# Local attention and two feed-forward networks on one core: the copies of the values all on GpSimd, other transfer costs in the plan, stores held behind attention's loads, and VectorE allowed to take differences

## The chip, the cores and the metric

One core of one Trainium2 chip runs the kernel. The metric is the device time of one execution in microseconds (us); lower is better. Times of one kernel are given as the median of several runs, and one further execution is recorded by the profiler.

## The reference, cut to what is computed

```python
# attention: batch 4, heads 8, 512 local and 32 global tokens, head_dim 64, window 32
s_g = scale * q_g @ k_all.T          # global queries see every key
out_g = softmax(s_g) @ v_all
s_ll = where(|i - j| <= 32, scale * q_l @ k_l.T, -1e9)
a_l = softmax(concat(scale * q_l @ k_g.T, s_ll))
out_l = a_l @ concat(v_g, v_l)
x = concat(out_g, out_l) as 2176 rows (tokens) of 512 (heads x head_dim)
# two networks, d_model 512, d_ff 2048
h = x @ w_in;  x = (h * cos(h)) @ w_out
h = max(x @ w2_in, 0);  out = (h * h) @ w2_out
```

The weights come as eight-byte floats (the kernel reads each as two 32-bit words), all else as four-byte floats.

## The kernel before, in words

**Attention.** Sixteen pairs of heads (pair p belongs to group p // 2, that is four heads of one batch). For each pair TensorE transposes keys and queries (tiles `tk`, `tq`), multiplies scores (`s`), transposes the probabilities (`tw`, and `tg` for the part of the global keys) and multiplies them with the values: first `o<-vgz` (global values), then `o<-va` and `o<-vb` in turn, line 459. The queries of 64 rows see a window of 128 keys, so half of the windows start in the middle of a 128-row block. `va` holds a group's values as loaded; `vb` holds the same values shifted by 64 rows, so that those windows lie at partition 0. `copy_v` makes `vb` from `va`: two copies of 64 x 1024 elements. For groups below `GVB` GpSimd makes them (line 288, rows `vb<-va`), for the others two transfers in the SyncE queue (line 252). `va` and `vb` have two buffers each, so group g waits until group g-2 is done. The gathers `pg<-pt` (line 412) also run on GpSimd; `tg` waits for them.

**Networks.** Each product is done with two-part numbers: a rounded high part (`ACTIVATE`, ScalarE) and the low part, the difference of value and high part (`split`, line 147, a `TENSOR_TENSOR` with both inputs in SBUF). Such differences are made of x (`xs`), of the weights (`wi`, `wo`) and of the middle values (`g`). There are 48 steps, each of 256 of d_ff and a block of 640 or 768 tokens: seven products `ha`, `hb`, `he` (line 820, a Strassen scheme), four middle values named a, d, e, b, then the jobs `y` (line 912), which need the high and low parts of g; the first jobs of a step need d and e. 24 steps belong to each network. At the start of each network the seven operands of each block of tokens are made (sums `xr`, line 683, and their parts `xs`) and stored to DRAM (line 706), from where later steps load them (line 711). The weights of a block come as `raw`, are converted (lines 115 to 138, on GpSimd, ScalarE and VectorE) and split.

**Who decides the order.** The order of attention on TensorE is a table written by hand. Everything else is placed by a planner inside the kernel: every operation is an `Op` with the engines that may do it and a duration on each, and a loop takes, engine by engine, the one that can start and has the earliest due time `latest` ("Q" is the queue of transfers, SyncE). The engines then run their instructions in the order thus written; an instruction that waits holds back all behind it on its engine or queue. `opG` makes an operation of GpSimd alone, `opVG` one for GpSimd or VectorE, whichever the planner finds earlier:

```python
    def opVG(n, fn, *needs):
        if beside[0]:
            return Op({"G": 0.1 + n * 0.0026, "V": 0.2 + n * 0.002}, ...)
```

`made_early` are the networks' operations that the planner may place within attention.

Of the kernel before, what the change touches and what calls it, by code (L numbers as in the profile page):

```python
# [20 lines left out]
P = 128  # L21
# [6 lines left out]
def kernel(  # L28
# [45 lines left out]
    V, A, G = nc.vector, nc.scalar, nc.gpsimd  # L74
# [173 lines left out]
    def copy_v(gi, eng="Q"):  # L248
        va, vb = VA[gi % 2], VB[gi % 2]
        for dst, src in ((vb[0:64], va[64:128, 0:4]), (vb[64:128], va[0:64, 1:5])):  # L250
            if eng == "Q":
                nc.sync.dma_start(dst, src)
            else:
                copy(eng, dst, src)
# [467 lines left out]
    d_g2 = lambda n: 0.1 + n * 0.00235  # L722
# [33 lines left out]
    def opG(d, fn, *needs):  # L756
        return Op({"G": d}, lambda e: fn(), *needs)

    def opVG(n, fn, *needs):
        if beside[0]:  # L760
            return Op({"G": 0.1 + n * 0.0026, "V": 0.2 + n * 0.002}, lambda e: fn(V if e == "V" else G), *needs)
        o = Op({"G": d_g2(n), "V": d_v2(n)}, lambda e: fn(V if e == "V" else G), *needs)
        o.port = "GV"
        return o
# [28 lines left out]
    class Step:  # L793
# [42 lines left out]
        def unit(self, ready, key, f, th):  # L836

            n, s = self.n, self.s
            h = lambda: self.hold(key)
            j, free = cr_ring.next()  # L840

            def new_r():
                self.r[key] = pools["s"].tile([P, 384], F32, tag=f"cr{j}", name="cr")[:, 0:n]
                return self.r[key]

            def ck():
                t = pools["s"].tile([P, 384], I32, tag=f"ck{i}", name="ck")
                self.r["k" + key] = t[:, 0:n]
                A.activation(self.r["k" + key], h(), AF.Copy, bias=0.25, scale=INV2PI)

            def cr():
                V.scalar_tensor_tensor(  # L852
                    new_r(), h(), INV2PI, self.r["k" + key], op0=ALU.mult, op1=ALU.subtract
                )

            def sin():
                A.activation(self.r[key], self.r[key], AF.Sin, bias=halfpi, scale=TWOPI)  # L857

            def relu():
                A.activation(new_r(), h(), AF.Relu)  # L860

            def gg():
                V.tensor_tensor(self.r[key], h(), self.r[key], op=ALU.mult)  # L863

            def ghi():
                if (s, f) not in GT:
                    GT[s, f] = [
                        pools["g"].tile([P, 768], F32R, tag=f"g{f}{i}{s % 2}", name=f"g{i}")
                        for i in range(2)
                    ]  # L870
                A.activation(GT[s, f][0][:, th * n : th * n + n], self.r[key], AF.Copy)  # L871

            def glo(eng):
                hi, lo = GT[s, f]
                c = slice(th * n, th * n + n)
                split(eng, lo[:, c], self.r[key], hi[:, c])

            if self.net == 0:
                i, kfree = ck_ring.next()
                o = opA(d_act(n), ck, ready, *kfree)  # L880
                o = opV(d_ps(n), cr, o, *free)
                ck_ring.free[i] = [o]
                o = opA(d_act(n) + 0.12, sin, o)
            else:
                o = opA(d_act(n), relu, ready, *free)
            o = opV(d_ps(n), gg, o)
            bank_free[self.bank[key]] = o
            o = opA(d_act(n), ghi, o, close_l, *g_free.get(s - 2, []))
            o = opG(d_g2(n), lambda: glo(G), o)
            cr_ring.free[j] = [o]  # L890
            self.half[key] = o

# [243 lines left out]
    q_in, q_at = {}, {}  # L1136
# [11 lines left out]
    def dma(fn, n, kb, *needs):  # L1148

        o = Op({"Q": 0.53 * n}, fn, *needs)  # L1150
        o.dmas = [kb / 205.0] * n
        return o

    def soft(fn, *needs):
# [5 lines left out]
    def opE(on, fn, *needs):  # L1160
        return Op(on, fn, *needs)
# [34 lines left out]
    def copy_vals(gi):  # L1196
        o, free = q_in["v", gi], vb_free.get(gi - 2, [])
        if gi < GVB:
            q_in["vb", gi] = Op({"G": 2.6}, lambda e: copy_v(gi, e), o, *free)
        else:  # L1200
            q_in["vb", gi] = dma(lambda e: copy_v(gi), 2, 256, o, *free)

# [94 lines left out]
    def scores(p):  # L1297
        x, r = pairs[p], p % 3
        main, wins, glob, fst, *qe = X[p]
        kt_free[r] = []  # L1300
        s = opP("S", 1.07, x.s_mm, main, wins, glob, *qe, *(o for k in s_bank.values() for o in k))
        qt_free[r] = [s]
        ep_ops.append(s)
        kt_free[r] = [s, fst]
        x.pg_op = {}
        slots = {}
        for hb in range(2):
            slots[hb] = tw_pt.next()
        for k in s_bank.values():
            k.clear()  # L1310
        kpg, fpg = pg_ring.next()
        x.pt_slot, x.pg_slot, x.pgs = {hb: slots[hb][0] for hb in range(2)}, kpg, PG[kpg]
        for hb in range(2):
            x.pt[hb] = PT[slots[hb][0]]
        x.st_slot, st_free = st_ring.next()
        x.st = ST[x.st_slot]
        todo = [(hb, i, h) for hb, i in ROUNDS for h in range(2)]
        exps = {0: [], 1: []}
        for hb, i, h in todo:
            done = soft(lambda: None, s)  # L1320
            done.lag = 0.27 * (ROUNDS.index((hb, i)) + 1)
            o = opE({"V": 0.245}, lambda e, a=(hb, i, h): x.top(*a), done, *slots[hb][1], *st_free)
            s_bank[UNIT[hb, i, h][0]].append(o)
            ep_ops.append(o)
            exps[hb].append(opE({"A": 0.411}, lambda e, a=(hb, i, h): x.exp(*a), o))
        x.rc = opE({"V": 0.42}, lambda e: x.recip(), *exps[0], *exps[1])
        x.exps = exps
        for hb in range(2):
            x.pg_op[hb] = opE({"G": 0.38}, lambda e, hb=hb: x.gather(hb), *exps[hb], *fpg)

    def p_tr(p, hb):

# [98 lines left out]
    def join(*ops):  # L1431
        return Op({"N": 0.0}, lambda e: None, *ops)

    GVB = 4

    ORDER = (
# [116 lines left out]
    for o in made_early:  # L1553
        o.latest -= 40
        if "Q" in o.on and hasattr(o, "raw"):
            o.latest -= 30

    missing = {o.key: len(o.needs) for o in allops}
    ready = {e: [] for e in "PVAGQN"}
# [19 lines left out]
    def best(e):  # L1579
# [20 lines left out]
                return (tw, w) if tw <= tp + 0.1 else (tp, p)  # L1600
            return (tp, p) if tp <= tw + 0.3 else (tw, w)
        f = free_at[e]
        if not ready[e]:
            return None
        t = max(f, min(o.at for o in ready[e]))
        can = [o for o in ready[e] if o.at <= t]
        o = min(can, key=lambda o: (o.latest, o.key))
        if e in "VAG":
            if not o.att:
# [31 lines left out]
        return t, o  # L1641

    port, lanes, way = [0.0], [0.0] * 8, [17.0]
    SLACK = 1.0
    BIAS, EARLY, LOOK, drift = 6.0, -100, 1, [0.0]
    count = len(allops)
    while count:
        picks = [(b[0], e, b[1]) for e in ready for b in [best(e)] if b]
# [8 lines left out]
        if e == "Q":  # L1657


            f = t  # L1660
            for d in o.dmas:
                f = max(f, lanes.pop(0)) + 0.53
                way[0] = max(way[0], f) + d
                lanes.append(way[0] + 2.2)
            o.end, free = lanes[-1], f
# [59 lines left out]
```

## Time and profile before

| | |
|---|---|
| median of 3 runs | 860.58 us (859.93 to 860.8) |
| the profiled execution's own time | 861.01 us |
| its span, first to last instruction | 859.2 us |
| TensorE busy in the span | 838.9 us (98%) |
| GpSimd, VectorE, ScalarE busy | 557.0, 635.5, 532.9 us |
| mean granted TensorE clock | 0.995 of full speed |

The span is 1.8 us shorter than the profiled execution's own time, which is 0.43 us above the median. Busy times count the time in which an engine works; engines overlap, so the sum is more than the span. PE is TensorE's matmuls, PEld its weight loads, DVE VectorE, ACT ScalarE, POOL GpSimd, SPq the SyncE queue that issues transfers.

### The profile page before, as it was taken

How to read it: one execution, taken by the hardware profiler on the slowest of the kernel's cores; microseconds unless marked ns; L12 is line 12 of the kernel's file. 1: busy time of each engine (PE TensorE's matmuls, PEld its weight loads, DVE VectorE, ACT ScalarE, POOL GpSimd, SP SyncE). 2: the span in 40 equal slices, each digit the busy share in tenths (PEclk: the TensorE clock that was granted, in tenths of full speed). 3: DMA queues.
4: the chain of work that ended last, by engine and by line, in shares of the span. 5: the costliest groups of instructions: out<-in, count | busy, mean ns of one | idle time of the engine just before them, and what ended most of it. 6: DMA issues, size and time to landing. Idle time of an engine off the chain costs nothing.

```text
span 859.2 us, 17102 instructions
## 1 busy us (share of the span) xinstructions
PE 838.9 (98%) x6100; PEld 778.5 (91%) x6100; DVE 635.5 (74%) x1398; ACT 532.9 (62%) x1268; POOL 557.0 (65%) x583
## 2 busy tenths in 40 slices
PE   8987998999999999999999999999999999999997
PEld 7876877999999999999999997889898989898986
DVE  6876898888887687769786999977746686454544
ACT  6987998886765566565655785756535554443331
POOL 4565889999765576458565999976726675431221
PEclk9999999999999999999999999999999999999999
DMA  9888944656685378538654745676764676446732
GB/s 173 187 203 217 231 120 180 268 178 226 254 325 180 121 300 300 162 124 339 244 177 150 281 165 216 220 276 231 247 214 179 246 285 194 138 166 233 227 117 79
DMA packets 133396, 179.89 MB, mean 209 GB/s; under 512 B 60608, under 2 KB 114368, under 8 KB 133312
## 3 DMA queue, kind: packets, MB, share of 16 engines
q1 hardware_dynamic: 129616, 177.63, 62.3%
q10 hardware_dynamic: 3696, 1.18, 0.6%
q8 instruction: 48, 0.79, 0.4%
q14 instruction: 36, 0.29, 0.1%
HBM read 141.03 MB, written 35.65 MB: 206 GB/s over the span
## 4 chain that ended last, share of the span: by engine, by line
PE 85%; POOL 6%; DMA 3%; ACT 2%; issue 1%; SPq 1%; DVE 1%; ACTq 0%; POOLq 0%
PE y L912 42%; PE hb L820 15%; PE he L820 10%; PE ha L820 10%; POOL xs L147 2%; POOL g L147 1%; PE s L368 1%; PE o L459 1%; PE tw L421 1%; POOL wf L138 1%; DMA qn<-in_q_l_dram 1%; ACT pt L393 1%; PE sg L503 1%; POOL wo L147 1%; PE o L444 1%
## 5 line engine op out<-in xcount | busy, mean ns | idle before, releaser
L147 POOL TENSOR_TENSOR g<-cr,g 128x384 fp32r<-128x384 f32 (+1 forms) x192 | 200.9, 1056 | 172.4 <-ACT g L871 159.0
L923 DVE TENSOR_TENSOR xt<-y,xt 128x384 f32<-128x384 f32 (+2 forms) x287 | 170.7, 596 | 102.5 <-PE y L912 100.6
L912 PE MATMUL y<-g,wo 128*128 128x384 f32 (+1 forms) x1152 | 217.8, 327 | 1.6 <-POOL g L147 1.6
L912 PE MATMUL y<-wo,g 128*128 128x512 f32 x816 | 210.4, 394 | 2.1 <-POOL g L147 2.1
L912 PEld LDWEIGHTS y<-g,wo 128*128 128x128 f32 x1152 | 193.8, 188 | 2.3 <-POOL g L147 2.3
L912 PEld LDWEIGHTS y<-wo,g 128*128 128x128 f32 x816 | 150.5, 188 | 26.6 <-POOL g L147 2.6
L820 PE MATMUL hb<-xs,wi 128*128 128x384 f32 (+1 forms) x864 | 167.0, 328 | 2.0 <-DVE hd L834 1.1
L820 PEld LDWEIGHTS hb<-xs,wi 128*128 128x128 f32 x864 | 147.8, 189 | 8.3 <-DVE hd L834 1.4
L820 PE MATMUL he<-xs,wi 128*128 128x384 f32 (+1 forms) x576 | 110.9, 327 | 0.1
L820 PE MATMUL ha<-xs,wi 128*128 128x384 f32 (+1 forms) x576 | 110.6, 326 | 0.2 <-ACT ptg L525 0.2
L871 ACT ACTIVATE g<-cr 128x384 fp32r<-128x384 f32 (+1 forms) x192 | 95.1, 503 | 19.8 <-DVE cr L863 19.4
L820 PEld LDWEIGHTS he<-xs,wi 128*128 128x128 f32 x576 | 98.1, 188 | 4.6 <-DVE cr L863 0.5
L138 POOL TENSOR_TENSOR wf<-wf,cc 128x512 uint32<-128x512 uint32 x64 | 86.9, 1357 | 22.4 <-DVE wf L126 15.0
L820 PEld LDWEIGHTS ha<-xs,wi 128*128 128x128 f32 x576 | 97.6, 188 | 2.4 <-ACT ptg L525 0.5
L857 ACT ACTIVATE cr<-cr,halfpi 128x384 f32<-128x384 f32 (+1 forms) x96 | 56.5, 593 | 14.7 <-DVE cr L852 13.9
L131 DVE SCALAR_TENSOR_TENSOR cc<-raw,cc 128x512 uint32<-128x512 uint32 x64 | 64.7, 1013 | 0.0
L393 ACT ACTIVATE pt<-pt,st 128x160 f32<-128x160 f32 x128 | 53.0, 418 | 3.7 <-DVE st L380 3.6
L147 POOL TENSOR_TENSOR wi<-ws,wi 128x512 fp32r<-128x512 f32 x27 | 36.2, 1339 | 24.1 <-ACT wi L171 12.7
L126 DVE TENSOR_SCALAR wf<-wf 128x512 uint32<-128x512 uint32 x64 | 49.6, 777 | 2.3 <-POOL wf L117 2.0
L828 ACT ACTIVATE s<-hb 128x384 f32<-128x384 f32 (+1 forms) x48 | 22.7, 474 | 46.0 <-PE hb L820 45.9
L828 ACT ACTIVATE s<-he 128x384 f32<-128x384 f32 (+1 forms) x48 | 22.7, 473 | 39.9 <-PE he L820 39.7
L122 ACT ACTIVATE cc<-raw 128x512 uint32<-128x512 uint32 x64 | 42.6, 668 | 1.1 <-POOL wf L138 1.1
(148 smaller groups left out, 1258.6 us busy)
## 6 DMA issues: line engine op xcount, KB each, us to landing
xs<-xs_T SPq DMA_DIRECT2D x48, 768.0 KB, 5.5
xs<-xs_B SPq DMA_DIRECT2D x36, 768.0 KB, 5.6
raw<-in_moe_w_in_dram SPq DMA_DIRECT2D x32, 512.0 KB, 5.1
raw<-in_moe_w_out_dram SPq DMA_DIRECT2D x32, 512.0 KB, 4.5
xs<-xs_T SPq DMA_DIRECT2D x24, 640.0 KB, 5.7
xs_T<-xs SPq DMA_DIRECT2D x16, 768.0 KB, 3.9
xs<-xs_B SPq DMA_DIRECT2D x18, 640.0 KB, 5.6
xs_B<-xs SPq DMA_DIRECT2D x12, 768.0 KB, 3.9
```

Of the source, the lines that this page charges most:

```text
L122: A.activation(v, raw[q, m, c][:, :, 0].bitcast(U32), AF.Copy, scale=2.0**-29)
L126: V.tensor_scalar(u, u, 3, None, op0=ALU.logical_shift_left)
L131: V.scalar_tensor_tensor(v, t[:, :, 1].bitcast(U32), 0x80000000, v, op0=ALU.bitwise_and, op1=ALU.bitwise_or,)
L138: G.tensor_tensor(u, u, v, op=ALU.add)
L147: eng.tensor_tensor(lo, x, hi.bitcast(F32), op=ALU.subtract)
L393: nc.scalar.activation(self.pt[hb][:, u, :], self.pt[hb][:, u, :], AF.Exp, bias=self.st[:, 0, 4 * hb + u : 4 * hb + u + 1], scale=-1.0, ac ...
L820: nc.tensor.matmul(out, lhsT=w[:, ws, c : c + P], rhs=xs[:, xh, kk, 0:n], start=start and k == 0, stop=k == 5, skip_group_check=True,)
L828: A.activation(self.sb[name], self.hold(bank_name), AF.Copy)
L857: A.activation(self.r[key], self.r[key], AF.Sin, bias=halfpi, scale=TWOPI)
L871: A.activation(GT[s, f][0][:, th * n : th * n + n], self.r[key], AF.Copy)
L912: nc.tensor.matmul(o, lhsT=l, rhs=r, start=k == 0, stop=k == 5)
L923: V.tensor_tensor(dst, y, dst, op=ALU.add)
```

## The change

`glo`, the low part of g, becomes an `opVG`: VectorE or GpSimd. `GVB` goes from 4 to 8: GpSimd copies the values of all eight groups, and the eight transfers `vb<-va` are gone. In the planner a transfer of attention costs kb/180 (kb/330 when over 200 KB) where it cost kb/205, a copy on GpSimd 2.1 where it cost 2.6, a gather 0.32 (0.38). As long as loads of attention are left, the queue Q takes a transfer of the networks only if its due time is within 30 us of TensorE's planned time. The weights' loads get due times 10 us earlier.

```diff
-            o = opG(d_g2(n), lambda: glo(G), o)
+            o = opVG(n, glo, o)
...
         o = Op({"Q": 0.53 * n}, fn, *needs)
-        o.dmas = [kb / 205.0] * n
+        o.dmas = [kb / (330.0 if kb > 200 else 180.0)] * n
...
         if gi < GVB:
-            q_in["vb", gi] = Op({"G": 2.6}, lambda e: copy_v(gi, e), o, *free)
+            q_in["vb", gi] = Op({"G": 2.1}, lambda e: copy_v(gi, e), o, *free)
         else:
             q_in["vb", gi] = dma(lambda e: copy_v(gi), 2, 256, o, *free)
...
-            x.pg_op[hb] = opE({"G": 0.38}, lambda e, hb=hb: x.gather(hb), *exps[hb], *fpg)
+            x.pg_op[hb] = opE({"G": 0.32}, lambda e, hb=hb: x.gather(hb), *exps[hb], *fpg)
...
-    GVB = 4
+    GVB = 8
...
         if "Q" in o.on and hasattr(o, "raw"):
-            o.latest -= 30
+            o.latest -= 40
...
-        if not ready[e]:
+        mine = ready[e]
+        if e == "Q" and aloads[0]:
+
+            mine = [o for o in mine if o.att or o.latest < free_at["P"] + HOLD]
+        if not mine:
             return None
-        t = max(f, min(o.at for o in ready[e]))
-        can = [o for o in ready[e] if o.at <= t]
+        t = max(f, min(o.at for o in mine))
+        can = [o for o in mine if o.at <= t]
...
+    HOLD = 30.0
+    aloads = [sum('Q' in o.on for o in attention)]
...
+            aloads[0] -= o.att
```

All of this moves instructions on every engine but leaves the instructions themselves: TensorE has the same matmuls in both. Counted over the whole program, 71 of the 192 differences g stand on VectorE in the changed kernel (none before), the copies `vb<-va` on GpSimd go from 8 to 16, and the queue has 8 transfers fewer. Three places follow.

**The SyncE queue, before group 4's values** (`va_93`, the second time this buffer is filled again). Before, two stores of `xs` stand ahead of them, and the copies `vb_95` behind two sets of queries and keys:

```order
L262 DMA vgz_97<-in_v_g_dram 32x4x64 x4
L706 DMA xs_0_B_1249<-xs 128x1536
L706 DMA xs_0_B_1261<-xs 128x1536
L240 DMA va_93<-in_v_g_dram 32x4x64
L243 DMA va_93<-in_v_l_dram 96x4x64
L243 DMA va_93<-in_v_l_dram 128x4x64 x3
L243 DMA va_93<-in_v_l_dram 32x4x64
L233 DMA qn<-in_q_l_dram 128x4x64 x4
L233 DMA kn<-in_k_l_dram 128x4x64 x4
L262 DMA vgz_98<-in_v_g_dram 32x4x64 x4
L252 DMA vb_95<-va_93 64x1024 x2
```

The changed kernel, from the same `vgz_97`:

```order
L262 DMA vgz_97<-in_v_g_dram 32x4x64 x4
L240 DMA va_93<-in_v_g_dram 32x4x64
L243 DMA va_93<-in_v_l_dram 96x4x64
L243 DMA va_93<-in_v_l_dram 128x4x64 x3
L243 DMA va_93<-in_v_l_dram 32x4x64
L92 DMA raw<-in_moe_w_in_dram 128x4x256
L233 DMA kn<-in_k_l_dram 128x4x64 x4
L233 DMA qn<-in_q_l_dram 128x4x64 x4
L706 DMA xs_0_B_1499<-xs 128x1536
```

The two stores (768 KB each) now stand behind group 4's values, and no transfer makes the copy; ahead of `vgz_97` both queues have the same number of transfers and bytes.

**GpSimd, at pair 8** (the first of group 4; `pg_117` takes its gathers). Before:

```order
L160 TENSOR_TENSOR ws<-wf_764,ws 128x256
L288 TENSOR_SCALAR kT_100<-kgT 128x32
L412 TENSOR_SCALAR pg_117<-pt_109 128x2x2x32
L138 TENSOR_TENSOR wf_1130<-wf_1130,cc 128x512
L412 TENSOR_SCALAR pg_117<-pt_110 128x2x2x32
L288 TENSOR_SCALAR kT_100<-kT_100 128x7x64
```

The changed kernel:

```order
L160 TENSOR_TENSOR ws<-wf_725,ws 128x256
L138 TENSOR_TENSOR wf_1052<-wf_1052,cc 128x512
L288 TENSOR_SCALAR vb_95<-va_93 64x1024 x2
L412 TENSOR_SCALAR pg_117<-pt_109 128x2x2x32
L412 TENSOR_SCALAR pg_117<-pt_110 128x2x2x32
L288 TENSOR_SCALAR kT_100<-kT_100 128x7x64
```

The two copies stand ahead of the pair's gathers, and they wait for the loads of `va_93`.

**GpSimd and VectorE, at step 25** (the second step of the second network; its low parts are `g_7329` and `g_7315` before, `g_7326` and `g_7352` in the changed kernel). GpSimd before, up to e, its second difference here, for which the first job waits:

```order
L138 TENSOR_TENSOR wf_7257<-wf_7257,cc 128x512
L147 TENSOR_TENSOR xs<-xt,xs 128x384
L138 TENSOR_TENSOR wf_7302<-wf_7302,cc 128x512
L147 TENSOR_TENSOR wo<-wf_7257,wo 128x512
L147 TENSOR_TENSOR wo<-wf_7302,wo 128x512
L147 TENSOR_TENSOR g_7315<-cr,g_7314 128x384
L147 TENSOR_TENSOR g_7329<-cr,g_7328 128x384
```

GpSimd in the changed kernel, up to d:

```order
L683 TENSOR_TENSOR xr<-xt 128x384
L138 TENSOR_TENSOR wf_7256<-wf_7256,cc 128x512
L147 TENSOR_TENSOR xs<-xt,xs 128x384
L138 TENSOR_TENSOR wf_7279<-wf_7279,cc 128x512
L147 TENSOR_TENSOR g_7352<-cr,g_7351 128x384
```

VectorE in the changed kernel, with e and the two differences of `wo`:

```order
L126 TENSOR_SCALAR wf_7279<-wf_7279 128x512
L863 TENSOR_TENSOR cr<-hd,cr 128x384
L147 TENSOR_TENSOR xs<-xt,xs 128x384
L147 TENSOR_TENSOR wo<-wf_7256,wo 128x512
L147 TENSOR_TENSOR g_7326<-cr,g_7325 128x384
L147 TENSOR_TENSOR xs<-xr,xs 128x384
L147 TENSOR_TENSOR wo<-wf_7279,wo 128x512
```

The difference e and both of `wo` have left GpSimd for VectorE.

## Rows read from the trace of the kernel before

**Rows 1.** The page, engines: busy us, share of the span, instructions.

```profile
PE 838.9 (98%) x6100; PEld 778.5 (91%) x6100; DVE 635.5 (74%) x1398; ACT 532.9 (62%) x1268; POOL 557.0 (65%) x583
```

**Rows 2.** Waits of TensorE: who for whom, us in total, times, longest.

```profile
PE o L459 <- DMA vb<-va: 4.2, 1, 4.2
PE y L912 <- POOL g L147: 3.8, 3, 2.1
PE tqg L274 <- DMA qgn<-in_q_g_dram: 1.3, 1, 1.3
...
PE tg L426 <- DMA kn<-in_k_l_dram: 0.6, 1, 0.6
```

**Rows 3.** Stretches: length; busy us of PE, PEld, DVE, ACT, POOL; PEclk; DMA; GB/s.

```profile
70.00:90.00 20.00, 15.57 (x257) 13.23 (x258) 12.40 (x62) 14.73 (x51) 10.60 (x17) 0.91 0.84 193
90.00:126.00 36.00, 35.53 (x648) 28.32 (x646) 31.70 (x151) 35.05 (x128) 30.28 (x44) 1.00 0.65 169
126.00:196.00 70.00, 66.43 (x476) 62.25 (x472) 62.29 (x107) 59.40 (x128) 69.84 (x65) 1.00 0.58 214
493.00:526.00 33.00, 30.89 (x171) 28.87 (x170) 30.96 (x39) 23.98 (x46) 33.00 (x27) 1.00 0.51 177
200.00:493.00 293.00, 293.00 (x1785) 293.00 (x1784) 230.22 (x433) 187.95 (x390) 191.89 (x183) 1.00 0.64 226
530.00:844.00 314.00, 314.00 (x1622) 282.31 (x1621) 199.71 (x314) 151.81 (x316) 171.84 (x164) 1.00 0.60 208
```

**Rows 4.** Short stretches of the same view behind TensorE's three longest waits.

```profile
82.00:84.00 2.00, 2.00 (x33) 1.88 (x34) 0.85 (x2) 0.00 (x0) 0.00 (x0) 0.66 1.21 271
84.00:86.00 2.00, 2.00 (x12) 2.00 (x11) 0.24 (x1) 1.27 (x3) 0.66 (x1) 0.50 1.17 203
...
180.00:200.00 20.00, 18.56 (x112) 18.24 (x111) 16.96 (x26) 14.96 (x32) 20.00 (x20) 1.00 0.74 250
...
526.00:528.00 2.00, 2.00 (x6) 1.67 (x7) 2.00 (x3) 0.74 (x1) 2.00 (x2) 0.60 0.41 169
528.00:530.00 2.00, 2.00 (x8) 1.95 (x7) 2.00 (x4) 1.01 (x3) 2.00 (x3) 0.55 1.02 415
```

**Rows 5.** TensorE in order of time: start, us, instruction [idle before, releaser].

```profile
82.00 0.24 PE L459 MATMUL o<-vb,tws 128*64 128x64 f32 x1 [4.23 <-DMA vb<-va]
...
196.46 0.96 PE L912 MATMUL y<-g,wo 128*128 128x384 f32 x4 [1.44 <-POOL g L147]
...
526.00 1.77 PE L912 MATMUL y<-wo,g 128*128 128x512 f32 x4 [2.12 <-POOL g L147]
```

**Rows 6.** The SyncE queue in order of time.

```profile
62.57 0.90 SPq L706 DMA_DIRECT2D xs_B<-xs  x2
...
64.51 5.65 SPq L243 DMA_DIRECT2D va<-in_v_l_dram  x5
...
77.36 1.19 SPq L252 DMA_DIRECT2D vb<-va  x2
```

**Rows 7.** GpSimd in order of time.

```profile
56.15 2.16 POOL L288 TENSOR_SCALAR vb<-va 64x1024 f32<-64x1024 f32 x2 [2.57 <-DMA va<-in_v_l_dram]
...
84.54 0.66 POOL L117 TENSOR_SCALAR wf<-raw 128x512 f32<-128x512 f32 x1 [3.02 <-DMA raw<-in_moe_w_in_dram]
87.14 0.56 POOL L288 TENSOR_SCALAR kT<-kT 128x448 f32<-128x448 f32 x1 [1.94 <-DVE kT L286]
```

**Rows 8.** A group of GpSimd by shape: busy us, mean ns, idle before.

```profile
L147 POOL TENSOR_TENSOR g<-cr,g 128x384 fp32r<-128x384 f32 x128 | 138.0, 1088 | 130.8 <-ACT g L871 117.8 <-PE y L912 12.7
```

**Rows 9.** Two differences on VectorE in order of time.

```profile
149.16 0.61 DVE L147 TENSOR_TENSOR xs<-xt,xs 128x384 fp32r<-128x384 f32 x1
...
150.74 1.30 DVE L147 TENSOR_TENSOR xs<-xr,xs 128x384 fp32r<-128x384 f32 x1
```

**Rows 10.** GpSimd at the same time.

```profile
149.32 1.33 POOL L147 TENSOR_TENSOR xs<-xt,xs 128x384 fp32r<-128x384 f32 x1
150.61 1.01 POOL L147 TENSOR_TENSOR xs<-xr,xs 128x384 fp32r<-128x384 f32 x1
```

More of the change, by code (lines that the diff above doesn't have):

```diff
@@ L1643 @@
     port, lanes, way = [0.0], [0.0] * 8, [17.0]
+    HOLD = 30.0
+    aloads = [sum('Q' in o.on for o in attention)]
     SLACK = 1.0
-    BIAS, EARLY, LOOK, drift = 6.0, -100, 1, [0.0]
+    BIAS, EARLY, LOOK, drift = 6.0, -100, 1.0, [0.0]
     count = len(allops)
```

## The prediction, made before the changed kernel was run

> **What bounds the kernel now.** I read the engines' totals first, then who TensorE waits for, then the totals by stretch, and last the order of time around each wait.
>
> TensorE is busy 838.9 us of a span of 859.2 [rows 1]. The matmuls are the same in the changed kernel, so it can gain only in the 20.3 us without a matmul and in matmuls that ran at a lower clock. Between 200 and 493 us and between 530 and 844 us TensorE is busy for the whole stretch at full clock [rows 3]: 607 us in which nothing can be gained. What is left lies in attention, in the passage to the first network and in the passage to the second.
>
> The list of waits names them: 4.2 us for the transfers that make `vb`, 3.8 us in three waits for differences g on GpSimd, 1.3 us for the global queries, 0.6 us at a transpose of gathers [rows 2]. In order of time the long ones end at 82.00 (4.23 us), 196.46 (1.44) and 526.00 (2.12) [rows 5]. Two of them cost more than they last: after TensorE has stood still for 4.23 us the granted clock is 0.66 and then 0.50 for two us each, after the 2.12 us 0.60 and 0.55 [rows 4]; 0.50 is the lower of its two levels, 1.2 GHz in place of 2.4. The loss is 2 x (0.34 + 0.50) = 1.7 us, and 2 x (0.40 + 0.45) = 1.7 us. Behind the 1.44 us wait the clock stays at 1.00 [rows 4]. So the first stall costs 4.2 + 1.7 = 5.9 us, the third 2.1 + 1.7 = 3.8, the second 1.4.
>
> The reader is to see a second thing: from 126 to 196 us GpSimd is busy 69.84 of 70 us, from 493 to 526 all 33 [rows 3]. There GpSimd paces the program, with TensorE just behind it. In 70 to 90 us it is busy 10.60 of 20 only.
>
> **The copies of the values.** The stall at 82 us is a queue, not a slow transfer: the two transfers are issued only at 77.36 [rows 6], about when TensorE needs them, since queries, keys and `vgz` stand ahead. They go. In their place GpSimd makes two copies, 2.16 us together [rows 7], as soon as group 4's values have landed. Those loads lose two stores ahead of them: the stores took 0.90 us to issue, and the five loads behind them 5.65 us [rows 6], against some 0.5 us for one issue elsewhere (0.90 us for two stores), so they were held up by the 1.5 MB in flight. Issued from 62.6 us at 0.5 to 0.7 us each they are out by about 66 us, and land about 70 us (estimate). Copies and gathers are then done about 73 us, and the multiplication with `vb` begins 77.7 us (82.00 less 4.23). The slack is some 4 us. I take the whole stall as gone: **-5.9 us** (bounds: nothing, if the loads land as late as 77 us, and -5.9).
>
> For groups 5 to 7 the same copies add 3 x 2.16 = 6.5 us to GpSimd between 85 and 120 us, where it has 36 - 30.28 = 5.7 us idle [rows 3]. That is the price, and it is paid later (below).
>
> **Smaller waits in attention.** The 0.6 us wait at `tg` follows the copy of group 3, which itself waited 2.57 us for its values [rows 7]; in the changed queue these loads stand four transfers further forward, so I take it as gone. The global queries have as many transfers and bytes ahead as before; that wait (1.3 us) I leave. **-0.6 us** (bounds 0 and -1.9). One product of the first network moves from between two pieces of attention's last pair to behind them; the gap that it filled may show: **+0.3 us** (bounds 0 and the product's own length, about 1.0).
>
> **The passage to the first network.** Will GpSimd let TensorE arrive 6.2 us earlier (5.9 + 0.6 - 0.3) at the job that now resumes at 196.46? Counted along GpSimd's order up to the last difference that this job needs from GpSimd (before: e of step 3; changed: d, as e is on VectorE), the changed kernel has eight copies more (+8.6 us), eight differences g fewer (8 x 1.09 = -8.7 us [rows 8]), and small exchanges with VectorE among `xr`, `xs`, `wi`, `wo` and the conversion that sum to about +1.9: **+1.8 us of work** in all. Against it stands idle time of GpSimd that can go. Before 196 us it idles 9.4 us in 70 to 90, 5.7 in 90 to 126 and 0.2 in 126 to 196 [rows 3]. Of the 9.4, 3.02 + 1.94 = 5.0 lie in or just behind the stall [rows 7] and go with it; group 4's copies fill 2.2 more; of the 5.7 I take half, 2.9, since the rest are waits for ScalarE's exponentials. That is 10.1 us (bounds 5.0 and 15.1). GpSimd can be 10.1 - 1.8 = 8.3 us earlier (3.2 to 13.3). TensorE asks for 6.2, and for 7.6 without the 1.44 us wait. The margin is thin, so I take half of that wait as gone: **-0.7 us** (bounds: -1.4; or, at 3.2, a wait of 1.44 + 3.0 = 4.4 us with a clock loss of 1.7 as behind the other long waits, +4.7).
>
> **The passage to the second network.** TensorE resumes at 526.00 with e of step 25. Before, 25 instructions of GpSimd lie between the last difference of step 23 and this e, without a gap [rows 3]; by the mean of each shape they are 29.7 us. In the changed order 22 lie between the same point and d: 26.1 us, 3.6 less. Both of `wo` and e are on VectorE, which was busy 30.96 of 33 us [rows 3]; along its order, by the mean of each shape, the work from the last middle value of step 23 to e and the last `wo` is 28.8 us, and 31.3 us were done before up to 526, as it sheds sums in exchange. Both differences, 3.6 and 2.5 us, are more than the 2.12 us wait. I take it as gone, with its clock loss: **-3.8 us** (bounds 0 and -3.8).
>
> **What lies beside other work.** The other 63 differences g on VectorE: in 200 to 493 us VectorE is busy 230 of 293, in 530 to 844 us 200 of 314 [rows 3], so at 0.61 to 1.30 us each [rows 9] they fit; without that cover each would delay an evacuation by its length. The weights' earlier loads and the changed costs only set the order. The later stores are read back after 200 us only. Behind the waits of SyncE for the last values' buffers now stand the weights of the second block, which only step 1's jobs need. All these: 0.
>
> **Sum.** -5.9 - 0.6 + 0.3 - 0.7 - 3.8 = -10.7 us. The profiled execution's own 861.01 us becomes 850.3; it lay 0.43 above the median, so 849.9 for the median.
>
> **Rivals.** *VectorE and GpSimd hold each other up, and the passage to the second network still waits.* Differences on VectorE lasted 0.61 and 1.30 us [rows 9]; while the second ran, GpSimd had its own of 1.01 us from 150.61 [rows 10], and one of GpSimd's took 1.33 where VectorE had begun first. Both engines are full from 493 to 526 us, so work moved between them may free nothing: then the front gains 6.9 and the end of the list nothing, 860.58 - 6.9 = 853.7 us. Against it: the counts on both engines fall. The Trainium skill, page "SBUF — State Buffer", section "Who interferes with whom", states this as a rule: a VectorE instruction with two SBUF inputs contends with a GpSimd instruction that reads SBUF, and the second blocks until the first has finished. The pair of rows agrees with it.
>
> *GpSimd gives the front's gain back at 196 us.* If only the 5.0 us of the stall's own idle go, GpSimd is 3.2 us earlier, and the wait of 4.4 us with its clock loss leaves 6.2 - 4.7 = 1.5 us. With the second passage's 3.8: 860.58 - 5.3 = 855.3. For it: GpSimd's 69.84 of 70 us. Against: a queue with more ready work covers some of the waits for exponentials.
>
> *Both together:* 860.58 - 1.5 = 859.1, within what a measurement can tell from no change, which I take as 0.2% (1.7 us).
>
> *Slower: the gathers queue behind copies that wait.* In groups 4 to 7 the copies stand ahead of gathers that TensorE's `tg` needs. At group 3 the copy waited 2.57 us for its values, and `tg` 0.6 [rows 2, 7]: 2.0 us of lateness are free. If each group's values came 4 us after GpSimd reaches the copy, `tg` would wait 2.0 us each time, and lose 1.7 us of clock as at 526: 4 x 3.7 = 14.8 us, less the 10.7 us gained, +4.1: 864.7 us. It decides from a lateness of about 3.7 us in every group. Against it: the loads stand further forward in the queue, and buffers of groups 6 and 7 are free before.
>
> **How the numbers follow.** Forecast 0.44, own range 847 to 853; first rival 0.22; second 0.12; both 0.11; slower 0.11. The predicted time is the forecast's, 849.9 us. The lowest sum is -5.9 - 1.9 - 1.4 - 3.8 = -13.0, 847.6; so 847 to 859.5 leaves out the slower case and some of the both-case, under 2 in 10. Faster 0.44 + 0.22 + 0.12 = 0.78, same 0.11, slower 0.11.
>
> **What the changed profile would show.** No wait of TensorE for `vb` and a clock of 1.00 throughout 70 to 90 us; copies `vb<-va` on GpSimd that end before TensorE's `o<-va` of the group begins. At the first job of step 3, now near 189 us, a wait under 1.4 us. At the first job of step 25, near 515 us, none, and a clock of 1.00 behind it. TensorE busy for all of the stretches between. I would be wrong if `tg` waits for gathers at the first pair of groups 4 to 7, if the wait at step 3 is over 2 us, or if TensorE waits for VectorE inside a network.

## The result, and the profile after

| | before | changed |
|---|---|---|
| median, us | 860.69 (4 runs, 859.93 to 860.98) | 849.46 (4 runs, 849.1 to 853.12) |
| profiled execution, its span | 861.01, 859.2 | 849.41, 847.6 |
| ratio of the times, 95% interval | | 0.9881 (0.9853 to 0.9908) |

The changed kernel is faster by 1.2%; 849.9 us were forecast. A second measurement of it gave 0.9873 (0.9852 to 0.9894). The page of the changed kernel, engines, against [rows 1]:

```profile
PE 834.6 (98%) x6100; PEld 776.8 (92%) x6100; DVE 662.1 (78%) x1445; ACT 532.0 (63%) x1271; POOL 524.1 (62%) x541
```

TensorE is busy 4.3 us less with the same matmuls, most of it the 3.4 us that it lost at the lower clock, and idle 13.0 us in place of 20.3. Whom it waits for, against [rows 2]:

```profile
PE ha L820 <- DVE cr L863: 1.9, 1, 1.9
PE hb L820 <- ACT s L828: 1.6, 1, 1.6
...
PE he L820 <- DVE cr L863: 0.6, 1, 0.6
```

The waits for `vb`, for `qgn` and for g are gone from the list. What leads it now are waits for VectorE and ScalarE in step 0, 4.1 us together. Step 0 had waits before too, but 2.0 us together (0.60, 0.31 and 1.08 us, for ScalarE's `xt` and `s` and VectorE's `hd`). By stretch, against [rows 3] (the passage to the second network is 12 us earlier than before, so 481 to 514 us answers to 493 to 526; the last row is the border itself):

```profile
70.00:90.00 20.00, 19.86 (x360) 15.96 (x358) 18.14 (x86) 19.64 (x71) 17.64 (x28) 1.00 0.96 243
90.00:126.00 36.00, 35.00 (x663) 28.72 (x661) 31.02 (x136) 34.42 (x123) 32.05 (x45) 1.00 0.44 143
126.00:196.00 70.00, 65.53 (x395) 64.04 (x386) 66.45 (x102) 58.54 (x118) 69.94 (x61) 1.00 0.61 215
481.00:514.00 33.00, 33.00 (x188) 31.51 (x187) 29.24 (x44) 23.59 (x45) 33.00 (x27) 1.00 0.62 225
514.00:520.00 6.00, 6.00 (x32) 5.38 (x31) 6.00 (x8) 4.17 (x10) 6.00 (x6) 1.00 0.53 216
```

From 70 to 90 us TensorE works 19.86 us in place of 15.57, at clock 1.00 in place of 0.91. Through the second passage it does not stop. TensorE in order of time, against [rows 5]:

```profile
127.34 0.33 PE L591 MATMUL tog<-ident,og_s 128*128 128x128 f32 x1 [0.38 <-DVE og_s L582]
...
132.54 1.33 PE L820 MATMUL hb<-xs,wi 128*128 128x384 f32 x6 [1.62 <-ACT s L828]
...
137.85 1.32 PE L820 MATMUL ha<-xs,wi 128*128 128x384 f32 x6 [1.88 <-DVE cr L863]
139.78 1.31 PE L820 MATMUL he<-xs,wi 128*128 128x384 f32 x6 [0.60 <-DVE cr L863]
...
189.39 1.03 PE L820 MATMUL ha<-xs,wi 128*128 128x320 f32 x6
...
515.39 1.55 PE L912 MATMUL y<-wo,g 128*128 128x512 f32 x6
...
519.21 1.21 PE L820 MATMUL he<-xs,wi 128*128 128x384 f32 x6
```

The same matmuls in the kernel before:

```profile
135.76 0.32 PE L591 MATMUL tog<-ident,og_s 128*128 128x128 f32 x1
...
197.26 1.03 PE L820 MATMUL ha<-xs,wi 128*128 128x320 f32 x6
...
523.26 0.63 PE L912 MATMUL y<-wo,g 128*128 128x512 f32 x2
...
531.03 1.23 PE L820 MATMUL he<-xs,wi 128*128 128x384 f32 x6
```

The two give the account. The last transpose of attention, `tog`, was at 135.76, now 127.34: 8.4 us earlier. One product of 1.05 us moved behind it, so attention itself takes 7.4 us less. The `ha` at 189.39, behind the job that waited 1.44 us, stood at 197.26: 7.9 earlier. The job at 515.39 began at 523.26 before, 7.9 us later as well, and its last four matmuls then stood until 526.00. What follows it is 11.8 us earlier (`he`, 531.03 before, 519.21 now): the second passage gave 4.0. The span is 11.6 us shorter.

GpSimd, against [rows 7], shows why: group 4's copies begin at once when their turn comes, 7.7 us ahead of the first `o<-vb` (76.69):

```profile
67.61 1.28 POOL L138 TENSOR_TENSOR wf<-wf,cc 128x512 uint32<-128x512 uint32 x1
68.98 2.16 POOL L288 TENSOR_SCALAR vb<-va 64x1024 f32<-64x1024 f32 x2
71.22 0.67 POOL L412 TENSOR_SCALAR pg<-pt 128x128 f32<-128x128 f32 x2
```

### The profile page after: what moved, and what is told of

It reads as the page before. It is cut to its first block, busy times and chain, and to the rows that moved or that the text cites. A ratio compares the mean times of both kernels' runs of the same rounds, so it can differ in the third digit from the quotient of the medians.

```text
span 847.6 us, 17019 instructions
## 1 busy us (share of the span) xinstructions
PE 834.6 (98%) x6100; PEld 776.8 (92%) x6100; DVE 662.1 (78%) x1445; ACT 532.0 (63%) x1271; POOL 524.1 (62%) x541
## 4 chain that ended last, share of the span: by engine, by line
PE 92%; ACT 3%; DVE 1%; POOL 1%; issue 1%; SPq 0%; DMA 0%; DVEq 0%; ACTq 0%; POOLq 0%
PE y L912 45%; PE hb L820 16%; PE he L820 11%; PE ha L820 11%; PE s L368 2%; ACT pt L393 1%; PE o L459 1%; PE tw L421 1%; PE spin L650 1%; PE o L444 1%; PE sg L503 1%; DVE pt L380 1%; PE tk L310 1%; PE tq L319 1%; PE og L572 1%
## 5 line engine op out<-in xcount | busy, mean ns | idle before, releaser
L147 POOL TENSOR_TENSOR g<-cr,g 128x384 fp32r<-128x384 f32 (+1 forms) x121 | 130.4, 1081 | 185.9 <-ACT g L871 168.9
L138 POOL TENSOR_TENSOR wf<-wf,cc 128x512 uint32<-128x512 uint32 x64 | 91.1, 1425 | 21.9 <-DVE wf L126 20.1
L147 POOL TENSOR_TENSOR wi<-ws,wi 128x512 fp32r<-128x512 f32 x31 | 42.7, 1381 | 35.3 <-ACT wi L171 25.1
L147 DVE TENSOR_TENSOR g<-cr,g 128x384 fp32r<-128x384 f32 (+1 forms) x71 | 54.0, 763 | 8.7 <-ACT g L871 8.3
L126 DVE TENSOR_SCALAR wf<-wf 128x512 uint32<-128x512 uint32 x64 | 47.6, 747 | 0.6 <-POOL wf L117 0.6
```

What stands on the lines that cost most here:

```text
L126: V.tensor_scalar(u, u, 3, None, op0=ALU.logical_shift_left)
L138: G.tensor_tensor(u, u, v, op=ALU.add)
L147: eng.tensor_tensor(lo, x, hi.bitcast(F32), op=ALU.subtract)
```

## The experiments

Each was timed beside the kernel before, which scattered more in these runs (857 to 863 us), so ratios are compared. "Span" is that of the profiled execution; 859.2 is before's, 847.6 the changed kernel's.

| run | what it is | median us | ratio to before | span |
|---|---|---|---|---|
| a1_vb_by_queue | changed, `vb` of groups 4 to 7 by SyncE | 858.54 | 0.9971 (0.9947 to 0.9995) | 856.7 |
| a2_g_on_gpsimd | changed, its order, all g on GpSimd | 857.87 | 0.9965 (0.9951 to 0.9979) | 855.6 |
| b1_vb_on_gpsimd | before, its order, `vb` by GpSimd | 858.69 | 0.9968 (0.9952 to 0.9983) | 857.9 |
| b2_fill_stall | before, 6 fillers in the stall | 859.14 | 0.9977 (0.9965 to 0.9989) | 859.0 |
| c1_fill_13 | before, 13 fillers | 859.3 | 0.9986 (0.9971 to 1.0002) | 857.5 |
| c2_only_g | before + g, new plan | 855.1 | 0.9945 (0.9919 to 0.9971) | 852.4 |
| c3_only_copies | before + copies, new plan | 856.76 | 0.9963 (0.9950 to 0.9976) | 854.9 |
| d1_all_but_g | changed without g, new plan | 854.61 | 0.9928 (0.9904 to 0.9951) | 854.0 |
| e3_all_but_queue | changed without the queue's part | 854.91 | 0.9929 (0.9905 to 0.9953) | 854.1 |
| e4_changed_again | changed | 849.76 | 0.9873 (0.9852 to 0.9894) | 847.4 |
| e1_chain_first | changed, step 0's chain ahead | 850.47 | 0.9880 (0.9859 to 0.9901) | 848.1 |
| e5_chain_first_g | the same, mended | 850.73 | 0.9880 (0.9860 to 0.9901) | 847.3 |

**The copies' engine.** Two runs change nothing but who makes `vb` of groups 4 to 7, each in the order of one kernel:

```diff
# a1, in the changed kernel
-            q_in["vb", gi] = Op({"G": 2.1}, lambda e: copy_v(gi, e), o, *free)
+            q_in["vb", gi] = Op({"G": 2.1}, lambda e: copy_v(gi, e if gi < 4 else "Q"), o, *free)
# b1, in the kernel before
-            q_in["vb", gi] = dma(lambda e: copy_v(gi), 2, 256, o, *free)
+            q_in["vb", gi] = dma(lambda e: copy_v(gi, "G"), 2, 256, o, *free)
```

> The changed kernel's plan and order, but the copies vb<-va of groups 4 to 7 are issued as two transfers each by the SyncE queue, at the place at which GpSimd made them. Theory (the copies on GpSimd took the stall at pair 8 away): TensorE waits for the transfers of vb again, 3 to 6 us at pair 8 with its clock loss, and the time is 853 to 855.5 us. Rival (the stall went because the two stores no longer stand ahead of the values; the copies' engine does not matter): no wait for vb over 0.5 us, GpSimd is 8.6 us lighter, and the time is 847 to 849.5 us.

> The kernel before with its plan and order, but the copies vb<-va of groups 4 to 7 are made by GpSimd at the place of the transfers. Theory (the copies end the stall, but GpSimd then gives the gain back at the passage to the first network, as nothing lightens it): no wait for vb, attention 5.9 us earlier, and a wait at step 3's first job that is some 4.7 us longer than 1.44; 857 to 860 us. Rival (GpSimd has idle time enough): the wait at step 3 stays under 2 us, 854.5 to 855.5 us. Second rival (the values land too late behind the stores): the wait at pair 8 stays, now for GpSimd, 860 us or more.

In a1 TensorE waits for transfers again, less at group 4 than before and 4.64 us at group 5, with the clock at its lower level behind it (TensorE in order of time, then a short stretch):

```profile
78.14 0.27 PE L459 MATMUL o<-vb,tws 128*64 128x64 f32 x1 [1.29 <-DMA vb<-va]
...
96.81 0.37 PE L459 MATMUL o<-vb,tws 128*64 128x64 f32 x1 [4.64 <-DMA vb<-va]
```

```profile
98.00:100.00 2.00, 2.00 (x20) 1.88 (x17) 0.98 (x3) 0.00 (x0) 0.00 (x0) 0.50 0.13 24
```

The theory's mechanism holds and costs 9 us of span, more than it said: attention ends at 136.57, 9.2 us later than in the changed kernel, 5.9 of them in these two waits and some 2.8 at the lower clock behind the second. The rival (the stores alone) fails by its own terms, but it holds for a part: with the stores moved, 1.29 of the 4.23 us are left at group 4. In b1 no wait for `vb` is left, but the gathers now queue behind the copies on GpSimd (b1, TensorE, then GpSimd):

```profile
91.52 0.76 PE L426 MATMUL tg<-ident,pg 128*128 128x128 f32 x2 [1.79 <-POOL pg L412]
```

```profile
86.08 2.71 POOL L288 TENSOR_SCALAR vb<-va 64x1024 f32<-64x1024 f32 x2
88.87 1.27 POOL L147 TENSOR_TENSOR wo<-wf,wo 128x512 fp32r<-128x512 f32 x1
90.11 0.65 POOL L117 TENSOR_SCALAR wf<-raw 128x512 f32<-128x512 f32 x1
90.71 1.18 POOL L412 TENSOR_SCALAR pg<-pt 128x128 f32<-128x128 f32 x2
```

TensorE waits 3.5 us for gathers in attention, in five places, and attention's end is only 0.5 us earlier. The number fits the theory, but not its place: of the 5.9 us 5.4 were lost in attention, and only 0.9 behind it (1.25 us of wait for g at the first jobs, 0.20 before, and 1.70 at step 3, 1.44 before).

**The clock behind the stall.** Products `o<-vgz` that start the sum anew fill the time in which TensorE waited at pair 8:

```diff
         def v_mm(self, hb):
+            for _ in range(13 if (self.p, hb) == (8, 0) else 0):   # 6 in b2
+                self.g_again()
```

`g_again` issues the 16 products of line 444 once more.

> The kernel before, but at pair 8 the product o<-vgz is made six times more in the place of 3.6 of the 4.23 us for which TensorE waits for vb (each starts the sum anew, so the result is the same). Theory (TensorE's clock falls because it stood still): the granted clock stays at 1.00 from 82 to 86 us and what follows is 1.7 us earlier at attention's end; the total is 858.9 us, or 860.6 if GpSimd gives it back at 196 us. Rival (the clock falls there for another reason, or by the length of the whole stall): clock 0.66 and 0.50 again, attention's end unmoved, 860.6 us.

> The kernel before, but at pair 8 the product o<-vgz is made thirteen times more (0.30 us each, as the run with six showed), so that TensorE works through nearly all of the 4.23 us for which it waited for vb (each starts the sum anew, so the result is the same). Theory (the clock falls because TensorE stood still): the wait is under 0.5 us, the granted clock is 1.00 from 82 to 86 us, and attention's last tog is 1.7 us earlier, at 134.1; the total is 1.7 us less, 858.9 us, or unmoved if GpSimd gives it back at 196 us. Rival (the clock falls there for another reason): 0.66 and 0.50 again and nothing earlier.

Six took 0.44 us each, not the 0.60 reckoned, so 2.41 us of wait were left, the clock fell all the same (0.52 and 0.63 in the two stretches), and attention ended 0.15 us earlier. Thirteen took 0.42 us each, where c1's expectation has 0.30. They leave no wait, as this execution came to pair 8 at 75.81, before at 76.84 (c1, stretches, then TensorE; lines there are six further down):

```profile
82.00:84.00 2.00, 2.00 (x41) 1.93 (x42) 0.76 (x2) 0.30 (x1) 0.66 (x1) 1.00 1.22 228
84.00:86.00 2.00, 2.00 (x27) 1.83 (x29) 1.47 (x5) 2.00 (x5) 0.50 (x1) 1.00 0.68 159
```

```profile
134.11 0.32 PE L597 MATMUL tog<-ident,og_s 128*128 128x128 f32 x1
...
194.83 0.96 PE L918 MATMUL y<-g,wo 128*128 128x384 f32 x4 [1.44 <-POOL g L147]
```

The first `o<-vb` is at 81.93, before 82.00, yet attention ends 1.65 us earlier: the loss of 1.7 us is real, and standing still is its cause. The other executions bear it out: c1's ten have mean granted clocks of 0.997 to 0.999, while 16 of the 20 of the kernel before beside them have 0.993 to 0.995. And the wait at step 3 is 1.44 us as before, at a time 1.63 us earlier: GpSimd came along with attention. The timed ratios of b2 and c1 overlap, and b2's gain has nothing in its profile that answers to it. But that profile is of one of its slowest executions (860.77 us, mean clock 0.995); seven of its ten have 0.997 to 0.999 and take 857.80 to 859.74 us. That the six fillers kept the clock in those is likely, and not shown.

**One part alone, and all parts but one.** These take lines of the change's diff as they stand and plan anew: c2 only `opVG`; c3 only `GVB` and the costs of copy and gather; d1 all but `opVG`; e3 all but the transfers' costs, `HOLD` and the weights' due times.

> The kernel before with one part of the change, planned anew: the differences g may go to VectorE. Theory: the stall at pair 8 stays (4.2 us and its clock loss), the second passage's wait goes with its clock loss (3.8 us) and the first's 1.44 too; 855 to 857 us, most likely 855.5. Rival (VectorE and GpSimd hold each other up, work moved between them frees nothing): both waits stay, 859.5 to 861 us.

> The kernel before with one part of the change, planned anew: GpSimd copies the values of all eight groups, at the change's costs; the two stores still stand ahead of group 4's values. Theory (the values land late behind the stores and GpSimd's gathers queue behind the copy): no wait for vb, but TensorE waits 2 to 4 us for gathers (tg), and the second passage waits as before; 857 to 860 us. Rival (the copies alone take the stall away): no wait over 0.6 us between 70 and 120 us, and 854 to 855.5 us.

> The changed kernel without one part, planned anew: all differences g on GpSimd. Theory: attention runs as in the changed kernel (its end near 127.3 us), but without the g on VectorE both passages wait for GpSimd: the first 1 to 5 us, the second 2 us with a clock loss of 1.7; 853 to 858 us, most likely 854.5. Rival (the passages pass because the front is better placed, not by g): no wait for GpSimd over 0.5 us at steps 3 and 25, 849 to 850 us.

> The changed kernel without one part, planned anew: g on VectorE and all copies on GpSimd, but the transfers' costs, the hold of the networks' stores and the weights' due times as before, so the two stores stand ahead of group 4's values again. Theory (the queue's part is worth what lies between the copies alone and the kernel without g, some 2.5 us, all of it in attention, and the passages go through): waits for scores' and probabilities' copies and gathers in attention of 2 to 4 us as with the copies alone, none at steps 3 and 25, 851 to 853.5 us. Rival (the copies and g do all of it): 849 to 850 us. Second rival (without the queue's part the copies wait for their values and take the gathers with them): 855 us or more.

c2: the stall is there (4.67 us at 80.91), and TensorE passes both borders without a wait; the theory holds. d1 is its mirror: at step 25 TensorE waits 2.12 us for GpSimd again. But two things differ from what was expected. The wait at step 3 does not return, and no clock is lost behind the 2.12 us (d1, TensorE, then stretches):

```profile
103.27 0.59 PE L426 MATMUL tg<-ident,pg 128*128 128x128 f32 x2 [1.68 <-POOL pg L412]
...
522.43 1.19 PE L912 MATMUL y<-wo,g 128*128 128x512 f32 x4 [2.12 <-POOL g L147]
```

```profile
522.00:524.00 2.00, 1.57 (x8) 1.40 (x9) 2.00 (x2) 0.29 (x1) 2.00 (x3) 1.00 0.17 71
524.00:526.00 2.00, 2.00 (x11) 1.74 (x11) 2.00 (x4) 1.46 (x3) 2.00 (x3) 1.00 1.02 415
```

The 1.68 us at 103.27 come from a copy that found its values late in this execution: 1.59 and 0.53 us before its two halves, none in the changed kernel, whose order is the same there. The clock is lost at step 0 instead: behind the same waits as in the changed kernel `he` takes 2.29 us (1.31 there), and from 142 to 146 us the granted clock is 0.58. So this execution, the longest of d1's four, is 6.4 us longer than the changed kernel's for three reasons: some 2.8 us lie in attention, which ends at 130.13, some 1.7 in the clock, and only 2.1 in the wait for g.

In c3 and e3 the two stores stand ahead of group 4's values, and copies wait for values: 4.1 us in three places in c3, 9.0 in four in e3. GpSimd in e3:

```profile
72.51 2.16 POOL L288 TENSOR_SCALAR vb<-va 64x1024 f32<-64x1024 f32 x2 [1.49 <-DMA va<-in_v_l_dram]
74.76 0.30 POOL L412 TENSOR_SCALAR pg<-pt 128x128 f32<-128x128 f32 x1
...
87.99 2.44 POOL L288 TENSOR_SCALAR vb<-va 64x1024 f32<-64x1024 f32 x2 [4.48 <-DMA va<-in_v_l_dram]
90.51 0.30 POOL L412 TENSOR_SCALAR pg<-pt 128x128 f32<-128x128 f32 x1
```

TensorE's `tg` waits 0.81 us at 75.11, its `og` 1.14 at 88.22; attention ends at 132.88 in place of 127.34. In c3 TensorE waits more for ScalarE (`tws`, 1.11 us at 96.56) than for gathers (0.70), so c3's theory is half right, and e3's time lies between its theory and its second rival. In times, leaving out g costs 0.9928 - 0.9881 = 0.5%, leaving out the queue's part 0.9929 - 0.9881 = 0.5% (4 us each, the intervals some 0.25% wide on each side); g alone brings 0.55%, the copies alone 0.37%. Only 2.1 us of the former are seen as a wait for g. No part does it alone, and the copies give what was forecast only with the queue's part beside them. The queue's part alone was not run; a1 comes nearest to it.

**The same order with g taken back.**

```diff
-                split(eng, lo[:, c], self.r[key], hi[:, c])
+                split(G, lo[:, c], self.r[key], hi[:, c])
```

> The changed kernel's plan and order, but all 192 differences g are made by GpSimd (71 of them were VectorE's). Theory (the g on VectorE let both passages pass): between 130 and 190 us GpSimd gets 7 differences of 1.09 us more where it is full, so the first passage waits up to 7.6 us again, and e of step 25 is 1.1 to 2.1 us late with its clock loss; 852 to 861 us, most likely 857. Rival (the order of the plan did it, with VectorE as full as GpSimd): no new wait over 0.5 us, 849 to 850 us.

The time is the theory's; the waits are many small ones: 0.90 us for g at 192.59, 0.82 for `hb` at 516.90, 0.5 for x. Some 1.4 us are lost to the clock at step 0 (`he` and `hb` from 140.76 take 2.29 and 1.60 us, 1.31 and 1.20 in the changed kernel). At the first job of step 25, where the expectation has a wait, TensorE loses at most 0.4 us: `wo` is still VectorE's in this order, and TensorE comes to the job 5.1 us later than in the changed kernel (520.49). The run shows what 71 differences cost where GpSimd is full; d1, planned without them, is the fairer measure.

**The time given back behind attention.** In the changed kernel step 0 waits 1.62, 1.88 and 0.60 us while VectorE and ScalarE convert weights that are due at 188 us. Two runs write these conversions behind step 0's chain:

```diff
     placed.sort(key=lambda o: (o.start, o.key))
+    LATE = dict.fromkeys((1165, 1166, 1167, 1168, 1171, 1172, 1173, 1174), 138.9) | {1107: 132.0}
+    turn = {}
+    for o in placed:
+        turn[o.key] = max([o.start, LATE.get(o.key, 0.0)] + [turn[x.key] + 1e-5 for x in o.needs])
+    placed.sort(key=lambda o: (turn[o.key], o.start, o.key))
```

> The changed kernel with its plan, but eight instructions groups that convert weights due only at 188 us (ScalarE and VectorE, placed between 131 and 139 us) are issued behind step 0's first sums and sines, and the low part of wo of 1.5 us behind the sum hd. Theory (the 2.4 us that the changed kernel gives back after attention are urgent work of step 0 that stands behind work that is not urgent, on VectorE and ScalarE): the waits of 1.62 and 1.88 us at step 0 shrink by 2 to 3 us together, the first y begins near 140.5 in place of 143.0, and the time is 2 to 3 us under the changed kernel's, 846.5 to 847.5 us by the first measurement of it. Rival (VectorE and GpSimd, busy for all of 126 to 196 us, pace that stretch, so work put off there comes back as a wait at steps 1 to 3): the waits only move, and the time is the changed kernel's within 1 us.

> The changed kernel once more, beside the others on the same chip. All theories: 849 to 850 us where the kernel before takes 860.6, so a ratio of 0.987 to 0.990.

> As the run with step 0's chain first, mended where that one waited: GpSimd's part of the two conversions stands behind step 0's differences g (there it stood between them and waited 1.64 us for VectorE), the conversions are spread over 143 to 147 us, and one of the two g that the first y needs goes to VectorE, which stood idle then. Theory (the 2.4 us given back after attention are urgent work behind work that is not): the first y follows the products without the wait of 2.40 us, near 140.2 us, and the time is 2 us under the changed kernel's, 847.4 to 848.2 us, a ratio to before of 0.985 to 0.986. Rival (VectorE and GpSimd pace 126 to 196 us): new waits for g or for x's parts appear at steps 0 to 3, and the time is the changed kernel's within 0.7 us, a ratio of 0.987 to 0.989.

e5 has 143.2 to 146.5 in place of 138.9, and one g of step 0 on VectorE. In e1 the two waits shrink to 0.96 and 1.30, and the first jobs then wait 2.40 us for a g that stands behind a conversion on GpSimd. In e5 that is mended, and the wait comes in step 1 (e5, TensorE, then VectorE):

```profile
140.48 2.24 PE L912 MATMUL y<-g,wo 128*128 128x384 f32 x12
...
154.11 1.31 PE L820 MATMUL he<-xs,wi 128*128 128x384 f32 x6 [2.03 <-DVE cr L863]
```

```profile
147.12 0.80 DVE L131 SCALAR_TENSOR_TENSOR cc<-raw,cc 128x512 uint32<-128x512 uint32 x1 [0.19 <-issue]
147.85 1.23 DVE L126 TENSOR_SCALAR wf<-wf 128x512 uint32<-128x512 uint32 x1
149.01 0.55 DVE L852 SCALAR_TENSOR_TENSOR cr<-hd,ck 128x384 f32<-128x384 f32 x1
```

The first y begins 2.5 us earlier than in the changed kernel (0.4 of it from an earlier end of attention), and 14 us later only 0.3 are left (this `he` is at 154.45 there): the conversions now stand in front of step 1's `cr`. Both times are the changed kernel's. The rival holds in both tries: VectorE (66.45 of 70 us) and GpSimd (69.94) set the pace there, and an order that serves one step robs the next. No version beat the changed kernel.

## Why the prediction was right, step by step

**The copies of the values: right.** Forecast -5.9 for the stall and, with the smaller waits and the moved product, -6.2; attention itself gave 7.4. By 61 us the changed kernel is 0.9 ahead, by the first `to` behind the stall 6.7 (86.66 before, 79.96 now), so the stall gave 5.8. Some 0.7 us more came behind it and were not forecast. The copies found their values at 68.98 us without a wait; in d1 and a2 the same copies waited until 69.39 and 69.79, which is the "about 70" of the estimate. c1 measures the clock's part by itself: 1.65 us for the 1.7 of the sum. What the forecast did not say is how much the step hangs on the queue: b1, c3 and e3 make the same copies and end attention 0.5, 5.1 and 2.9 us earlier only, since copies wait for values or gathers for copies.

**Smaller waits: right, and one beside them that comes and goes.** The wait at `tg` went as forecast (with one of 0.33 us behind it: `sg` at 61.60 before, 60.67 now). The "+0.3" for the moved product showed too: the last `tog` waits 0.38 us, where it had no wait before.

The wait for the global queries, which the sum left in, is gone from the list, and yet nothing was gained: TensorE began 1.1 us later in the changed kernel's profile (`sg` of the first group at 17.17, before 16.06), met the transfer when it had landed, and both kernels are level at the next `sg` (46.61 and 46.56). An early start does not bring the wait with it, though. The changed kernel's second profile, e4, began as early as before (15.81), did not wait, and was 1.3 us ahead at the next `sg` (45.27); c1, with before's queue, began at 16.26 and did not wait either. The kernel before, then e4:

```profile
44.51 0.63 PE L274 MATMUL tqg<-ident,qgn 128*128 128x128 f32 x4 [1.28 <-DMA qgn<-in_q_g_dram]
```

```profile
42.91 0.60 PE L274 MATMUL tqg<-ident,qgn 128*128 128x128 f32 x4
```

So the queries had landed by 42.9 us in one execution and at about 44.5 in the other. Four more runs waited 0.34 to 0.65 us (a2, e5, d1, e3). What decides it is not shown.

**The passage to the first network: size nearly right, the reasoning wrong.** The step asked "Will GpSimd let TensorE arrive 6.2 us earlier", and counted its idle time and work from 70 us on, as if its end at 196 us stood fixed. c1 refutes that: TensorE 1.65 us earlier, GpSimd too, the wait at step 3 unmoved. The likely reason is that much of GpSimd's work in that stretch is made of attention's output, so it moves with attention's end. Nor is the 1.44 us g's affair alone: it is gone in d1 with every g on GpSimd. What the stretch does is trade waits. From the last `tog` to the first y it takes 15.7 us, and 12.9 before with one product of 1.05 us fewer: 1.7 us are lost at step 0, for which the sum has no term. From that y to the `ha` behind step 3's first job it takes 46.4 us, 48.6 before: 2.2 us are gained, the 1.44 among them. Together 0.5 us are gained, and 0.7 were forecast. One sign by which the prediction would be wrong did come: TensorE waits for VectorE inside a network, 1.88 and 0.60 us for `cr` at step 0 (before, 1.08 us for `hd`).

**The passage to the second network: right, in this execution.** -3.8 forecast, -4.0 measured. The cause is shown for the part as a whole: the wait is there in d1, where both `wo` and both g stand on GpSimd again (516.67 to 522.38), and not in c2. It is not shown for the engine of e alone, as a2 has all g on GpSimd, `wo` on VectorE and hardly a wait. And of the 3.8 only 2.1 are sure: the 1.7 of the clock came in before, b2, c1 and c3, and not in d1, nor in b1 behind 2.08 us.

**The rivals.** *Hold each other up*: the wait did not stay, but the effect is real. VectorE and GpSimd ahead of step 25 in the changed kernel:

```profile
510.71 0.83 DVE L147 TENSOR_TENSOR wo<-wf,wo 128x512 fp32r<-128x512 f32 x1 [1.85 <-ACT wo L180]
511.46 1.65 DVE L147 TENSOR_TENSOR g<-cr,g 128x384 fp32r<-128x384 f32 x1
```

```profile
510.95 1.75 POOL L138 TENSOR_TENSOR wf<-wf,cc 128x512 uint32<-128x512 uint32 x1
512.65 1.34 POOL L147 TENSOR_TENSOR g<-cr,g 128x384 fp32r<-128x384 f32 x1
```

Alone these take 0.56 (the median of the 71 g on VectorE) and 1.28 us (67.61 above). Read in turns: GpSimd stands until VectorE's `wo` is over at about 511.46 and works 1.28, to 512.74 (the row ends at 512.70); VectorE's g stands until then and works 0.56, to 513.26 (the row ends at 513.11). By the Trainium skill, page "SBUF — State Buffer", section "Who interferes with whom", a VectorE instruction with two SBUF inputs contends with a GpSimd instruction that reads SBUF, the port pair that they share is an exclusive lock, and the order of issue decides who blocks. The trace agrees within 0.15 us. By the counts on both engines, the passage went because they fell by more than this costs. *GpSimd gives the gain back at 196*: not there, for the reason above. *Slower*: its mechanism, gathers behind copies that wait, is what e3 and c3 show, with waits of up to 4.48 us; even so they are faster than before, since not every group was late by 3.7 us. In the changed kernel the queue's part keeps it away.

## What to carry to other kernels

A stall at a transfer is cured by who makes the data only if the input comes in time: put the loads forward and change the maker together, and test each alone. Do not count an engine's backlog as a clock of its own when its work is made of the waiting engine's output; ask what it would do if that output came earlier. A wait that ends with a transfer's landing can come and go between executions of one kernel, so its going in one pair of profiles says nothing of the change; look whether the matmuls behind it are really earlier. And where all helpers of a stretch are full, reordering moves the waits and takes work off no one.

## What was not expected of the hardware

The same wait of TensorE, 2.08 to 2.12 us at the first job of step 25, was followed by two stretches of 2 us at granted clocks of 0.50 to 0.66 and 0.50 to 0.70 in four executions (before, b2, c1, c3) and by 1.00 in two (b1, d1). At step 0 the waits of 1.6 and 1.9 us cost no clock in the changed kernel's first profile and about 1.3 us in its second (e4):

```profile
136.53 1.48 PE L820 MATMUL ha<-xs,wi 128*128 128x384 f32 x6 [1.90 <-DVE cr L863]
138.45 2.29 PE L820 MATMUL he<-xs,wi 128*128 128x384 f32 x6 [0.44 <-DVE cr L863]
```

```profile
138.00:142.00 4.00, 3.56 (x15) 3.55 (x15) 3.75 (x6) 3.12 (x8) 3.92 (x4) 0.63 0.58 181
```

In a2 and d1 `he` takes 2.29 us there as well. The mean granted clock of the kernel before differs in the same way from one execution to the next: 0.993 to 0.998 in the 31 beside a1. So a clock loss read behind a wait of about 2 us in one profile is a chance, not a price. What decides it in the execution was not found.
